# Loading k ahead of q in the head of an attention and shrink-MLP kernel, and storing its last block in quarters

## Chip, cores and metric

The kernel runs on one core of a Trainium2 chip. The metric is the device time of one execution in microseconds (us), as the median of several runs. A profile is one further execution with the hardware profiler on; its span goes from the first to the last instruction, and the execution's own time is a little longer.

## What is computed

Pooled attention for 8 batches of 8 heads, 576 rows, head width 64, and then a two-layer network without bias whose activation is `h - tanh(h)`:

```python
k_p = k.reshape(B, H, Sp, 8, D).mean(axis=3)      # 576 rows -> 72 pooled rows, v likewise
scores = q @ k_p.T / sqrt(D)
attn = exp(scores - max(scores)); attn /= sum(attn)
x = (attn @ v_p), heads side by side              # 4608 x 512
h = x @ w_in                                      # 512 -> 2048
out = (h - tanh(h)) @ w_out                       # 2048 -> 512
```

Inputs and output are float32; inside the kernel the products are of bf16 operands with float32 sums.

## The kernel before

**Tiling.** The rows are worked on in nine groups of 512: group g below 8 takes rows 0 to 511 of batch g (each partition holds four neighbouring rows, j = 0 to 3), and the ninth, g = 8, takes the 64 left-over rows ("tails") of all eight batches. For a group, TensorE first does the h-products (`h_mms`, 16 units of 128 hidden columns; for group 0 in half-wide pairs, `h_mm_pair`, line 447), ScalarE takes the tanh (`h_act`, line 438) and VectorE subtracts it (line 439) into `gT`; then the products with `w_out` follow (`o_mms`, line 468). The attention of batch g + 1 is fitted between them by a plan written out by hand (`plan`, lines 870 to 900).

**Three groups with seven products.** For g in `SEVEN` = (6, 7, 8) the second product is done as a 2 by 2 block product with seven instead of eight sub-products (`PRODUCTS`, line 530, in the order 4, 2, 7, 1, 6, 5, 3; each in two row blocks b = 0 and 1). It needs four sums of quarters of `gT`, S1 to S4 (`g_sum`, line 527). Products 4, 7, 1, 6, 5 and 3 run on in the same two PSUM banks, one for each b, and what is in the bank is copied out in between (`evacuate`, lines 554 to 572): so the copy after product 1 must have read the bank before product 6 adds to it. S2 and S4 are made on VectorE, S1 on GpSimd (line 960). `finish_11` (line 578) adds a last term to a quarter of the output, on GpSimd. `store_half` (line 593 for g = 8) stores columns `C1` (0 to 255) or `C2` (256 to 511), or both, of half hf of the rows, in two transfers.

**The head.** Everything before the steady state is written out by hand from line 605 to line 753, and each engine takes its instructions in that order. The loads of k and q of batch 0 are split into pieces: k in tiles of 128 rows, t = 0 to 4 (t = 4 has 64 rows, 128 KB; two tiles have 512 KB), q in pairs of j (512 KB for two). SyncE and ScalarE have issue queues of their own for them; v, the weights and batch 1's k and q are issued by GpSimd, which converts on the way where the target is bf16: v of batch 0 after the load of k tiles 0 and 1 (`after`, line 637), chunks 1 to 3 of `w_in` after the last step of pooling k (line 672). VectorE pools k (`pool_k`, lines 209 to 215); TensorE turns the pooled k and the q tiles by products with an identity (`turn`, line 272), and ScalarE or VectorE copies them out (`k_place`, line 246; `q_turn_pe`, line 652). Scores (`s_mms`, line 291) go to PSUM; `s_shift` (lines 303 and 306) takes the maximum and subtracts it on VectorE, and `s_exp` (line 342) takes one exponential over all eight heads. The other way, `s_max` with `s_exp_heads` (lines 311 to 332), gives ScalarE the negated maximum as a bias and takes one exponential for each head, straight from PSUM. E is turned on TensorE and copied out (`e_turn_pe`, line 361), multiplied with v (`av_mms`, line 378), normalised (lines 399 and 400) and turned again (`x_turn_pe`, line 417). `fill` (line 599) issues products of zeros that nothing reads.

**Batch 1 in the head.** GpSimd pools k of batch 1 (`pool_k(1, nc.gpsimd)`, line 736, about 6 us) and then converts q of batch 1 tile by tile (line 738). TensorE turns those q tiles from the ninth step of the loop at line 743 on (line 750).

Of the kernel before, what the change touches and what calls it, by code (L numbers as in the profile page):

```python
# [15 lines left out]
B, H, S, D = 8, 8, 576, 64  # L16
POOL = 8
G = S // POOL
DM, DFF = 512, 2048
NHP = H // 2  # L20
R = 4
QA = 128 * R
# [4 lines left out]
NG = 9  # L27
NT = 5
# [10 lines left out]
def kernel(  # L39
# [20 lines left out]
    def flat(b0, n):  # L60
        return PS[:, b0 : b0 + 2, :].rearrange("p k c -> p (k c)")[:, 0:n]
# [63 lines left out]
    def load_rows(src, dst, b, t0=0, t1=NT, eng=None):  # L125
        eng = eng or nc.sync
        r = []
        n1 = min(t1, 4)
        if t0 < n1:
            r.append(  # L130
                eng.dma_start(
                    out=dst[:, t0:n1, :],
                    in_=src[b, 128 * t0 : 128 * n1, :].rearrange("(t p) n -> p t n", p=128),
                )
            )
        if t1 == NT:
            r.append(eng.dma_start(out=dst[0:64, 4, :], in_=src[b, 512:NK, :]))
        return r

    def load_q(b, dst, j0=0, j1=R, eng=None):  # L140
        return (eng or nc.sync).dma_start(
            out=dst[:, :, j0:j1, :],
            in_=q[b, :, 0:QA, :].rearrange("h (p j) d -> p h j d", j=R)[:, :, j0:j1, :],
        )
# [51 lines left out]
    def after(lds, dep):  # L196
        for ld in lds:
            tc.add_manual_dep(
                ld.ins,
                dep.ins.name,  # L200
                mybir.DependencyInfo(mybir.DependencyClass.Sync, mybir.DependencyReason.DATA),
            )


    def pool_k(b, eng, t0=0, t1=NT):
        r = k_raw[b % 2].rearrange("p t (j d) -> p t j d", d=D)[:, t0:t1, :, :]
        kd = kds[b % 2][:, t0:t1, :, :]
        n = t1 - t0
        eng.tensor_tensor(  # L209
            out=r[:, :, 0:4, :], in0=r[:, :, 0:4, :], in1=r[:, :, 4:8, :], op=ALU.add  # L210
        )
        eng.tensor_tensor(
            out=r[:, :, 0:2, :], in0=r[:, :, 0:2, :], in1=r[:, :, 2:4, :], op=ALU.add
        )
        return eng.tensor_tensor(
            out=kd,
            in0=r[:, :, 0:1, :].to_broadcast([128, n, 2, D]),
            in1=r[:, :, 1:2, :].to_broadcast([128, n, 2, D]),
            op=ALU.add,
        )  # L220
# [38 lines left out]
    def q_cast(b, eng, j0=0, j1=R):  # L259
        eng(  # L260
            out=q_bf[b % 2][:, j0:j1, :, :].rearrange("p j h d -> p h j d"),
            in_=q_raw[b % 2][:, :, j0:j1, :],
        )
# [35 lines left out]
    def s_shift(banks):  # L299
        sc = two(banks, 4 * G).rearrange("p k (h c) -> p k h c", c=G)  # L300
        mx = work.tile([128, 2, 4, 1], FP32, name="mx", tag="mx")
        sh = work.tile([128, 2, 4, G], FP32, name="sh", tag="sh", bufs=4)
        nc.vector.reduce_max(  # L303
            out=mx.rearrange("p k h o -> p k (h o)"), in_=sc, axis=AX.X
        )
        nc.vector.tensor_tensor(  # L306
            out=sh[:, :, :, :], in0=sc, in1=mx.to_broadcast([128, 2, 4, G]), op=ALU.subtract
        )
        return sh
# [25 lines left out]
    def slot(n):  # L335
        return E_ps[n // 2 % 2], ET_ps[n // 2 % 2], n % 2
# [3 lines left out]
    def s_exp(sh, sl):  # L340
        E, ET, e = sl
        nc.scalar.activation(  # L342
            out=E[:, e, :, :].rearrange("p t c -> p (t c)")[:, 0:NK],
            in_=sh.rearrange("p k h c -> p (k h c)"),
            func=ACT.Exp,
            scale=SCALE,
        )
# [233 lines left out]
        o = o_hs[1][:, :, C2]  # L581
        eng.tensor_tensor(out=o, in0=o, in1=n0, op=ALU.subtract)

    def store_half(g, hf, cols=slice(0, DM), engs=(nc.sync, nc.sync)):
        o = o_hs[hf]
        if g < B:
            blk = out[g * S : g * S + QA, :].rearrange("(p j) m -> p j m", j=R)
            nc.sync.dma_start(out=blk[:, 2 * hf : 2 * hf + 2, cols], in_=o[:, :, cols])
            return
        tl = out.rearrange("(n t) m -> t n m", t=S)[QA:S, :, :]  # L590
        for e in range(2):
            n = 4 * hf + e
            engs[e].dma_start(
                out=tl[:, n : n + 3 : 2, cols], in_=o[64 * e : 64 * e + 64, :, cols]
            )

    def fill(n, bank, cols=512):
        for _ in range(n):
            nc.tensor.matmul(  # L599
                PS[:, bank, 0:cols], lhsT=zeros[:, 0:128], rhs=zeros[:, 0:cols], start=True, stop=True  # L600
            )
# [2 lines left out]
    ve, se, ge = nc.vector.tensor_copy, nc.scalar.copy, nc.gpsimd.tensor_copy  # L604
    nc.vector.memset(zeros[:, :], 0.0)
    nc.vector.memset(k_raw[0][64:128, 4, :], 0.0)
    k0 = load_rows(k_rows, k_raw[0], 0, 0, 2)
    load_q(0, q_raw[0], 0, 2, nc.scalar)
    k0 += load_rows(k_rows, k_raw[0], 0, 4, NT, nc.scalar)
    k0 += load_rows(k_rows, k_raw[0], 0, 2, 4)  # L610
    load_q(0, q_raw[0], 2, 4)
    nc.vector.memset(v_bf[0][64:128, 4, :], 0.0)
    nc.vector.memset(v_bf[1][64:128, 4, :], 0.0)
# [20 lines left out]
    nc.gpsimd.memset(mask[64:128, 4, :, :], 0.0)  # L634
    for i in range(3):
        nc.gpsimd.tensor_scalar_mul(VB[i][:, :, :, D:D1], mask[:, :, :, :], float(POOL))
    after(load_rows(v_rows, v_bf[0], 0, eng=nc.gpsimd), k0[0])
    w1_dmas = [load_w1(0)]
    nc.gpsimd.memset(k_raw[1][64:128, 4, :], 0.0)

# [1 line left out]
    def k_turn_pe(b, t0, t1, kps):  # L642
        for t in range(t0, t1):
            turn(kps[:, t * 128 : (t + 1) * 128], kds[b][:, t, :, :].rearrange("p a d -> p (a d)"))

    def q_turn_pe(b, j, bank, eng):
        for m in range(NHP):
            turn(
                PS[:, bank, m * 128 : (m + 1) * 128],
                q_bf[b % 2][:, j, 2 * m : 2 * m + 2, :].rearrange("p h d -> p (h d)"),  # L650
            )
        eng(out=qTs[b][:, j, :, :].rearrange("p m c -> p (m c)"), in_=PS[:, bank, :])

    def v_pool_pe(b, bank):
# [8 lines left out]
            )  # L663
        return vps

    pool_k(0, nc.vector, 0, 2)
    pool_k(0, nc.vector, 4, NT)
    pooled = pool_k(0, nc.vector, 2, 4)
    for c in range(1, 4):
        w1_dmas.append(load_w1(c))  # L670
# [4 lines left out]
    load_w2(0)  # L675
    load_w2(1)
    q_cast(0, se, 0, 2)
    q_cast(0, se, 2, 4)
    kps = flat(4, NT * 128)
    k_turn_pe(0, 0, 2, kps)  # L680
    k_turn_pe(0, 4, NT, kps)
    fill(3, 7)
    k_turn_pe(0, 2, 4, kps)
    k_place(0, kps[:, 0:NK], (ve, se))
    q_turn_pe(0, 0, 6, se)
    q_turn_pe(0, 1, 7, se)
    fill(2, 0)
    s_mms(s_block(0, 0), (0, 1))
    sh = [s_shift((0, 1))]
    s_mms(s_block(0, 1), (2, 3))  # L690
    sh.append(s_shift((2, 3)))
    vps = v_pool_pe(0, 6)
    v_place(0, vps, nc.vector)
    s_exp(sh[0], slot(0))
    fill(3, 7)
    e_turn_pe(slot(0), 4, se)
    s_exp(sh[1], slot(1))
    q_turn_pe(0, 2, 0, ve)
    fill(2, 7)
    e_turn_pe(slot(1), 2, se)  # L700
    q_turn_pe(0, 3, 1, se)
    av_mms(slot(0), av_block(0), (6, 7))
    xs = [x_pair(), x_pair()]
# [161 lines left out]
    for g in range(1, NG):  # L865
# [68 lines left out]
        for i in range(NHID):  # L934
            bk = HB[i // 2 % 3][i % 2] if g in SEVEN else i % 6
            h_mms(g, i, bk)
            if g in SEVEN and i == 15:
                for it in plan.pop(-1, ()):
                    step(*it)
            if i % 2:  # L940
                h_act(i - 1, bk - 1)
                if g in SEVEN:
                    if i in (3, 5) and carry:
                        carry.pop(0)()
                    for n, i0 in {13: [(3, 0)], 15: [(3, 4)]}.get(i, ()):
                        g_sum(n, i0, i0 + 4)
            for it in plan.get(i - NHID, ()):
                step(*it)
            if more and i in (13, 15):
                q_cast(nb + 1, se, i - 13, i - 11)  # L950
        for u in range(14 if g in SEVEN else 0):
            n, b = PRODUCTS[u // 2], u % 2
            product(n, b)
            evacuate(n, b, nb is not None)
            for it in plan.get(u, ()):
                step(*it)
                run_late()
            if u == 2:
                dep = g_sum(2, 0, NQ)
                after([g_sum(1, 0, 4, nc.gpsimd), g_sum(1, 4, NQ, nc.gpsimd)], dep)  # L960
            if u == 8:
                g_sum(4, 0, NQ)
            if b == 0:
                continue
            if n == "1":
                finish_11(nc.gpsimd, nb is not None)
                if g == NG - 1:
                    store_half(g, 0, C1)
            elif g == NG - 1 and n == "5":
                store_half(g, 1)  # L970
            elif g == NG - 1 and n == "3":
                store_half(g, 0, C2, (nc.sync, nc.scalar))
            elif n in "53":
                if n == "5" and nb is not None:
                    finish_22(nc.gpsimd)
                store_half(g, 0 if n == "3" else 1)
        if g in SEVEN and tail is not None:
            carry += [lambda i=tail: tail_values(i), lambda i=tail: x_turn_dma(x_tl, B, i, 1)]
        for u, (tb, qd) in enumerate(() if g in SEVEN else UNITS):
# [51 lines left out]
```

## Time and profile before

| what | value |
|---|---|
| median of three runs | 306.02 us (305.19 to 307.4) |
| the profiled execution | 306.24 us, its span 304.2 us |
| TensorE busy | 287.7 us, 95% of the span |
| VectorE, ScalarE, GpSimd busy | 202.8, 145.0 and 135.4 us |
| TensorE busy from 0 to 42 us | 33.77 us |
| TensorE busy from 100 to 220 us | 120 us of 120 |
| first h-product of group 0 | 22.27 us |
| TensorE's last products begin | 296.01 us |
| last store issued | 299.4 us |

How to read it: TensorE, VectorE, ScalarE and GpSimd are called PE, DVE, ACT and POOL in the rows, PEld is TensorE's loading of weights, SP is SyncE; a name with q, such as SPq, is that engine's queue of issuing instructions. A row of the timeline has its start, its duration (both in us), engine, line of the kernel, operation, written tile `<-` read tiles, shapes, a count, and in brackets how long the engine sat idle before and what ended that. A granted clock of 1.00 is TensorE's full clock.

### The profile page before, as it was taken

To read this page: it belongs to the slowest core of one execution; us is meant where nothing else is said; L and a number is where in the kernel's file an instruction comes from. 1 tells how busy PE (TensorE), PEld (TensorE's weight loads), DVE (VectorE), ACT (ScalarE), POOL (GpSimd) and SP (SyncE) were. 2 spreads that over 40 slices of the span, in tenths; PEclk is the share of its full clock that TensorE was granted. 3 is DMA by queue.
4 is the path that set the end of the run, shared out by engine and by line. 5 is a ranking of instruction groups with operands and counts; after the bars stand their busy time and mean duration, and the time that the engine had idled before them with its cause. 6 is when DMAs were issued, how large, how long until landed. Compare 5 with 4: busy or idle time off the path is not lost.

```text
span 304.2 us, 4875 instructions
## 1 busy us (share of the span) xinstructions
PE 287.7 (95%) x1885; PEld 164.0 (54%) x1885; DVE 202.8 (67%) x283; ACT 145.0 (48%) x199; POOL 135.4 (45%) x112
## 2 busy tenths in 40 slices
PE   5779989899999999999999999999999999999991
PEld 1357865444454455445544454455447854874681
DVE  4586866549853993398329942986699847656861
ACT  2457755347523762366237623672366336416520
POOL 7544918308810692088107910791062920250080
PEclk9599999999999999999999999999999999999998
DMA  7999996789899999896799799959825540021005
GB/s 226 224 218 319 207 290 161 136 254 331 169 218 186 357 180 192 251 314 114 177 254 322 136 155 270 337 63 219 241 65 72 91 160 17 2 99 43 1 0 138
DMA packets 85383, 54.84 MB, mean 180 GB/s; under 512 B 60240, under 2 KB 73168, under 8 KB 85360
## 3 DMA queue, kind: packets, MB, share of 16 engines
q1 hardware_dynamic: 77696, 44.84, 58.7%
q0 software_dynamic: 6400, 8.91, 14.2%
q10 hardware_dynamic: 1264, 0.79, 0.9%
q8 instruction: 14, 0.23, 0.3%
q14 instruction: 9, 0.07, 0.1%
HBM read 36.70 MB, written 9.44 MB: 152 GB/s over the span
## 4 chain that ended last, share of the span: by engine, by line
PE 80%; DVE 10%; DMA 3%; ACT 3%; issue 1%; ACTq 0%; DVEq 0%
PE PS L425 31%; PE PS L468 26%; PE PS L545 11%; PE PS L378 4%; DVE gT L439 3%; PE PS L447 3%; PE PS L291 3%; DMA k_raw<-in_k_dram 2%; DVE sh L306 2%; DVE mx L303 2%; PE PS L272 2%; DMA xT<-x_sb 1%; PE PS L599 1%; DVE x_sb L400 1%; ACT E L342 1%
## 5 line engine op out<-in xcount | busy, mean ns | idle before, releaser
L439 DVE TENSOR_TENSOR gT<-PS,t_sb 128x1024 bf16<-128x1024 f32 x64 | 77.1, 1220 | 42.8 <-ACT t_sb L438 42.8
L425 PE MATMUL PS<-xT,w1b 128*128 128x512 bf16 x448 | 100.8, 379 | 1.0 <-DMA xT<-x_sb 0.9
L468 PE MATMUL PS<-w2b,gT 128*128 128x512 bf16 x384 | 89.8, 379 | 0.2 <-ACT v_sm L782 0.2
L438 ACT ACTIVATE t_sb<-PS 128x1024 f32<-128x1024 f32 x64 | 65.6, 1024 | 49.8 <-PE PS L425 48.4
L425 PEld LDWEIGHTS <-w1b 128*128 128x128 bf16 x512 | 49.1, 98 | 57.6 <-issue 1.9
L468 PEld LDWEIGHTS <-gT 128*128 128x128 bf16 x384 | 35.3, 98 | 37.7 <-issue 0.5
L224 POOL TENSOR_TENSOR v_raw<-v_raw 128x1280 f32<-128x1280 f32 x6 | 17.4, 2906 | 40.8 <-DMA v_raw<-in_v_dram 40.8
L489 ACT COPY o_h<-PS 128x512 f32<-128x512 f32 x22 | 12.8, 584 | 45.9 <-PE PS L468 45.8
L527 POOL TENSOR_TENSOR q_raw<-gT 128x1024 bf16<-128x1024 bf16 x6 | 12.6, 2122 | 44.3 <-PE PS L545 38.5
L303 DVE TENSOR_REDUCE mx<-PS 128x8 f32<-128x576 f32 x36 | 26.9, 748 | 5.8 <-PE PS L291 5.8
L342 ACT ACTIVATE E<-sh 128x576 bf16<-128x576 f32 x32 | 21.8, 680 | 18.5 <-DVE sh L306 18.5
L306 DVE TENSOR_TENSOR sh<-PS,mx 128x576 f32<-128x576 f32 x36 | 27.3, 757 | 1.2
L400 DVE TENSOR_TENSOR x_sb<-PS,rden 128x512 bf16<-128x512 f32 x32 | 22.1, 691 | 1.1
L399 DVE RECIPROCAL rden<-PS 128x8 f32<-128x8 f32 x36 | 7.3, 204 | 22.8 <-PE PS L378 22.7
L209 POOL TENSOR_TENSOR k_raw<-k_raw 128x1280 f32<-128x1280 f32 x7 | 20.3, 2904 | 0.1
L545 PEld LDWEIGHTS <-q_raw 128*128 128x128 bf16 x192 | 18.5, 98 | 2.6 <-DVE q_raw L527 0.4
L246 POOL COPY KB<-kT 64x288 bf16<-64x288 bf16 x12 | 5.1, 422 | 28.6 <-DMA kT<-kd 22.6
L260 ACT CAST q_bf<-q_raw 128x1024 bf16<-128x1024 f32 x14 | 14.4, 1038 | 5.6 <-DMA q_raw<-in_q_dram 5.6
L378 PEld LDWEIGHTS <-ET 128*128 128x128 bf16 x192 | 13.2, 98 | 5.3 <-ACT ET L361 0.8
L378 PE MATMUL PS<-VB,ET 128*128 128x130 bf16 (+2 forms) x192 | 15.8, 221 | 0.2 <-ACT ET L361 0.2
L447 PE MATMUL PS<-xT,w1b 128*128 128x256 bf16 x128 | 15.3, 273 | 0.7 <-ACT xT L417 0.7
L545 PEld LDWEIGHTS <-gT 128*128 128x128 bf16 x144 | 13.9, 98 | 2.0
(95 smaller groups left out, 294.4 us busy)
## 6 DMA issues: line engine op xcount, KB each, us to landing
k_raw<-in_k_dram SPq DMA_DIRECT2D x14, 512.0 KB, 8.5
out_dram<-o_h SPq DMA_DIRECT2D x26, 256.0 KB, 3.1
v_raw<-in_v_dram SPq DMA_DIRECT2D x12, 512.0 KB, 5.0
q_raw<-in_q_dram SPq DMA_DIRECT2D x11, 512.0 KB, 7.0
w1b<-in_moe_w_in_dram POOLq DMA_DIRECT2D x4, 512.0 KB, 8.9
q_raw<-in_q_dram POOLq DMA_DIRECT2D x2, 1024.0 KB, 14.8
w2b<-in_moe_w_out_dram POOLq DMA_DIRECT2D x4, 512.0 KB, 18.9
out_dram<-o_h SPq DMA_DIRECT2D x4, 512.0 KB, 2.8
```

The lines of the kernel that those rows point to most:

```text
L209: eng.tensor_tensor(out=r[:, :, 0:4, :], in0=r[:, :, 0:4, :], in1=r[:, :, 4:8, :], op=ALU.add)
L303: nc.vector.reduce_max(out=mx.rearrange("p k h o -> p k (h o)"), in_=sc, axis=AX.X)
L306: nc.vector.tensor_tensor(out=sh[:, :, :, :], in0=sc, in1=mx.to_broadcast([128, 2, 4, G]), op=ALU.subtract)
L342: nc.scalar.activation(out=E[:, e, :, :].rearrange("p t c -> p (t c)")[:, 0:NK], in_=sh.rearrange("p k h c -> p (k h c)"), func=ACT.Exp, s ...
L378: nc.tensor.matmul(PS[ps, banks[half], D1 * h : D1 * (h + s1 - s0)], lhsT=ET[:, t, c0 : c0 + (ps.stop - ps.start)], rhs=VB[kb][:, t, s0:s1 ...
L400: nc.vector.tensor_tensor(out=x_sb, in0=ps[:, :, :, 0:D], in1=rden.to_broadcast([128, 2, 4, D]), op=ALU.mult,)
L425: nc.tensor.matmul(PS[:, bank, :].rearrange("p (j c) -> p j c", j=R), lhsT=w1b[:, fb, i * 128 : (i + 1) * 128], rhs=xT_of(g)[:, :, fb, :], ...
L438: nc.scalar.activation(out=t_sb[:, :, :], in_=ps, func=ACT.Tanh)
L439: nc.vector.tensor_sub(out=gT[:, i : i + 2, :], in0=ps, in1=t_sb[:, :, :])
L447: h_mm_last[0] = nc.tensor.matmul(PS[:, bank, 256 * s : 256 * s + 256].rearrange("p (j c) -> p j c", j=2), lhsT=w1b[:, fb, (2 * n + s) * 1 ...
L468: nc.tensor.matmul(PS[:, bank, 0 : c1 - c0], lhsT=gT[:, i, tb * 128 : (tb + 1) * 128], rhs=w2b[:, i, c0:c1], start=(i == 0), stop=(i == NH ...
L545: nc.tensor.matmul(ps, lhsT=A[:, i, 128 * b : 128 * b + 128], rhs=B_[:, i, :], start=(n in "24" and i == 0), stop=(i == NQ - 1), skip_grou ...
```

## The change

The loads of batch 0 are issued in another order: k tile 4 first on ScalarE's queue; k tiles 0 and 1, k tiles 2 and 3, q tiles 0 and 1 and q tiles 2 and 3 on SyncE's. Pooling and turning k start with tile 4. Of the zero products after the first nine, three of ten stay. The second q tile is copied out on VectorE, and q tiles 2 and 3 are converted there instead of on ScalarE. The first score block's exponential is taken head by head with the maximum as bias; the second block keeps `s_shift`. Pooling v comes after both exponentials in the program, and both E are turned one after the other. For g = 7 and 8 all sums S2, S1 and S4 are made on VectorE right after the last `h_act`. For g = 8 `finish_11` goes to VectorE, and the output is stored in quarters, the last one in two parts.

```diff
-    def store_half(g, hf, cols=slice(0, DM), engs=(nc.sync, nc.sync)):
-        o = o_hs[hf]
-        if g < B:
-            blk = out[g * S : g * S + QA, :].rearrange("(p j) m -> p j m", j=R)
-            nc.sync.dma_start(out=blk[:, 2 * hf : 2 * hf + 2, cols], in_=o[:, :, cols])
-            return
+    def store_half(g, hf):
+        blk = out[g * S : g * S + QA, :].rearrange("(p j) m -> p j m", j=R)
+        nc.sync.dma_start(out=blk[:, 2 * hf : 2 * hf + 2, :], in_=o_hs[hf][:, :, :])
+
+    def store_part(hf, cols, b0, b1, engs=(nc.sync, nc.sync)):
         tl = out.rearrange("(n t) m -> t n m", t=S)[QA:S, :, :]
         for e in range(2):
-            n = 4 * hf + e
+            n = 4 * hf + 2 * b0 + e
             engs[e].dma_start(
-                out=tl[:, n : n + 3 : 2, cols], in_=o[64 * e : 64 * e + 64, :, cols]
+                out=tl[:, n : n + 2 * (b1 - b0) - 1 : 2, cols],
+                in_=o_hs[hf][64 * e : 64 * e + 64, b0:b1, cols],
             )
...
-    k0 = load_rows(k_rows, k_raw[0], 0, 0, 2)
-    load_q(0, q_raw[0], 0, 2, nc.scalar)
-    k0 += load_rows(k_rows, k_raw[0], 0, 4, NT, nc.scalar)
+    k0 = load_rows(k_rows, k_raw[0], 0, 4, NT, nc.scalar)
+    k0 += load_rows(k_rows, k_raw[0], 0, 0, 2)
     k0 += load_rows(k_rows, k_raw[0], 0, 2, 4)
+    load_q(0, q_raw[0], 0, 2)
     load_q(0, q_raw[0], 2, 4)
...
-    after(load_rows(v_rows, v_bf[0], 0, eng=nc.gpsimd), k0[0])
+    after(load_rows(v_rows, v_bf[0], 0, eng=nc.gpsimd), k0[1])
...
+    pool_k(0, nc.vector, 4, NT)
     pool_k(0, nc.vector, 0, 2)
-    pool_k(0, nc.vector, 4, NT)
     pooled = pool_k(0, nc.vector, 2, 4)
...
     q_cast(0, se, 0, 2)
-    q_cast(0, se, 2, 4)
     kps = flat(4, NT * 128)
+    k_turn_pe(0, 4, NT, kps)
     k_turn_pe(0, 0, 2, kps)
-    k_turn_pe(0, 4, NT, kps)
-    fill(3, 7)
+    fill(2, 7)
     k_turn_pe(0, 2, 4, kps)
     k_place(0, kps[:, 0:NK], (ve, se))
     q_turn_pe(0, 0, 6, se)
-    q_turn_pe(0, 1, 7, se)
-    fill(2, 0)
+    q_turn_pe(0, 1, 7, ve)
+    q_cast(0, ve, 2, 4)
     s_mms(s_block(0, 0), (0, 1))
-    sh = [s_shift((0, 1))]
+    ng = s_max((0, 1))
     s_mms(s_block(0, 1), (2, 3))
-    sh.append(s_shift((2, 3)))
+    sh = [None, s_shift((2, 3))]
+    s_exp_heads((0, 1), ng, slot(0))
+    s_exp(sh[1], slot(1))
+    fill(1, 7)
     vps = v_pool_pe(0, 6)
     v_place(0, vps, nc.vector)
-    s_exp(sh[0], slot(0))
-    fill(3, 7)
     e_turn_pe(slot(0), 4, se)
-    s_exp(sh[1], slot(1))
+    e_turn_pe(slot(1), 2, se)
     q_turn_pe(0, 2, 0, ve)
-    fill(2, 7)
-    e_turn_pe(slot(1), 2, se)
     q_turn_pe(0, 3, 1, se)
     av_mms(slot(0), av_block(0), (6, 7))
...
                     for n, i0 in {13: [(3, 0)], 15: [(3, 4)]}.get(i, ()):
                         g_sum(n, i0, i0 + 4)
+                    if i == 15 and nb is None:
+                        for n in (2, 1, 4):
+                            g_sum(n, 0, NQ)
...
-            if u == 2:
+            if nb is not None and u == 2:
                 dep = g_sum(2, 0, NQ)
                 after([g_sum(1, 0, 4, nc.gpsimd), g_sum(1, 4, NQ, nc.gpsimd)], dep)
-            if u == 8:
+            if nb is not None and u == 8:
                 g_sum(4, 0, NQ)
-            if b == 0:
-                continue
-            if n == "1":
-                finish_11(nc.gpsimd, nb is not None)
-                if g == NG - 1:
-                    store_half(g, 0, C1)
-            elif g == NG - 1 and n == "5":
-                store_half(g, 1)
-            elif g == NG - 1 and n == "3":
-                store_half(g, 0, C2, (nc.sync, nc.scalar))
-            elif n in "53":
-                if n == "5" and nb is not None:
-                    finish_22(nc.gpsimd)
-                store_half(g, 0 if n == "3" else 1)
+            if g == NG - 1:
+                if n == "1" and b:
+                    finish_11(nc.vector)
+                    store_part(0, C1, 0, 2)
+                elif n == "6" and b:
+                    store_part(1, C1, 0, 2)
+                elif n == "5" and b:
+                    store_part(1, C2, 0, 2, (nc.sync, nc.scalar))
+                elif n == "3":
+                    store_part(0, C2, b, b + 1, (nc.sync, nc.scalar))
+            elif b:
+                if n == "1":
+                    finish_11(nc.gpsimd, nb is not None)
+                elif n in "53":
+                    if n == "5" and nb is not None:
+                        finish_22(nc.gpsimd)
+                    store_half(g, 0 if n == "3" else 1)
```

## The prediction

> **What bounds the kernel now.** I read the page first: TensorE is busy for 95% of the span, so only where it idles can this change act.
>
> ```profile
> PE   5779989899999999999999999999999999999991
> PEclk9599999999999999999999999999999999999998
> DMA  7999996789899999896799799959825540021005
> ```
>
> The digits of PE (7.6 us each) fall short in the first slices and in the last one. So I read the head and the tail, first by the windows view (PE busy, PEld, DVE, ACT, POOL, then granted clock, DMA share, GB/s).
>
> ```profile
> 6.00:8.00 2.00, 0.28 (x2) 0.11 (x2) 0.35 (x1) 0.79 (x1) 1.87 (x4) 1.00 1.09 297
> 8.00:10.00 2.00, 0.13 (x2) 0.13 (x3) 1.20 (x4) 0.26 (x1) 0.00 (x0) 0.59 1.23 259
> 12.00:14.00 2.00, 2.00 (x15) 1.10 (x13) 0.28 (x1) 1.47 (x3) 2.00 (x4) 0.50 1.24 205
> 14.00:16.00 2.00, 2.00 (x14) 1.38 (x12) 1.90 (x3) 0.35 (x1) 2.00 (x3) 0.70 1.24 201
> ```
>
> TensorE has nothing to do from 6 to 10 us, its clock is halved from 8.4 to 15.2 us, and the transfers are at their limit (share above 1). Then the timeline, head first.
>
> ```profile
> 8.74 0.43 DVE L209 TENSOR_TENSOR k_raw<-k_raw 128x256 f32<-128x256 f32 x1 [2.38 <-DMA k_raw<-in_k_dram]
> 22.27 1.03 PE L447 MATMUL PS<-xT,w1b 128*128 128x256 bf16 x8 [0.67 <-ACT xT L417]
> 27.41 0.74 POOL L192 DMA_DIRECT2D w2b<-in_moe_w_out_dram  x1 [2.56 <-DMA k_raw<-in_k_dram]
> 34.31 2.29 POOL L260 CAST q_bf<-q_raw 128x512 bf16<-128x512 f32 x4
> 36.77 0.39 PE L272 MATMUL PS<-ident,q_bf 128*128 128x128 bf16 x4
> ```
>
> k tile 4 lands at 8.7 us and holds the scores; the first h-product starts at 22.27. GpSimd waits for batch 1's k until 27.41, pools it, and converts batch 1's q from 34.31: each of the four takes 0.61, so the first is there at 34.92, and TensorE turns it at 36.77, 1.85 later. From 30 to 40 us TensorE is busy throughout. Last the tail.
>
> ```profile
> 288.78 1.22 DVE L527 TENSOR_TENSOR q_raw<-gT,q_raw 128x2048 bf16<-128x2048 bf16 x1
> 290.17 4.20 POOL L527 TENSOR_TENSOR q_raw<-gT 128x1024 bf16<-128x1024 bf16 x2 [19.66 <-PE PS L545]
> 292.01 0.42 DVE L572 TENSOR_TENSOR o_h<-PS,k_raw 128x256 f32<-128x256 f32 x1 [2.01 <-PE PS L545]
> 292.51 3.66 PE L545 MATMUL PS<-k_raw,q_raw 128*128 128x256 bf16 x32
> 293.13 2.33 DVE L527 TENSOR_TENSOR q_raw<-gT,q_raw 128x2048 bf16<-128x2048 bf16 x1
> 294.32 2.26 POOL L578 TENSOR_TENSOR o_h<-o_h,k_raw 128x512 f32<-128x512 f32 x1
> 296.61 3.56 SPq L593 DMA_DIRECT2D out_dram<-o_h  x5
> 297.96 0.42 DVE L572 TENSOR_TENSOR o_h<-PS,k_raw 128x256 f32<-128x256 f32 x1 [0.45 <-PE PS L545]
> ```
>
> The last copy ends at 298.38, but SyncE, held by GpSimd's addition until 296.6, issues stores one after the other until about 300.1, and the transfers run until about 302.7 (the windows view has 225 GB/s up to 302.5, 96 up to 303).
>
> **The change, part by part. Head, loads.** All of k and q of batch 0 come in 2.23 MB; by the DMA view 0.27 MB had come by 3 us, 0.90 by 5, 1.84 by 8, and the last packets at 9.5. The sum stays, the order changes. With k alone at some 0.36 MB/us (355 to 437 GB/s in the rows just before 3 us) tile 4 is there at about 3.3, tiles 0 and 1 at 4.2, 2 and 3 at 5.7; q at 0.29 MB/us (287 near 9 us): tiles 0 and 1 at 7.4, 2 and 3 between 9.5 and 10.5, later if v, now issued about 0.6 earlier, takes a share. SyncE issues four loads of 0.46 instead of three, ScalarE one instead of two: its table load moves forward by 0.5 and costs nothing, since ScalarE then waits for q.
>
> **Head, k and q.** VectorE pools tile 4 (1.03), tiles 0 and 1 (1.61), tiles 2 and 3 (1.60) from 3.3 on without a gap but for the landing: done at 7.6 instead of 11.3. Turn 0.3, the two copies of k 0.45 and 0.39: KB at 8.9 instead of 12.7. ScalarE's q cast (1.04) ends at 8.45, first q tile turned and copied (0.4 + 0.58) by 9.55, scores by 10.0 instead of 14.0.
>
> **Head, what VectorE gains.** Ahead of the maximum now stand the copy of the second q tile (0.68) and the cast of q tiles 2 and 3, which waits for that last load. Behind this wait stand the maximum, the second block's two steps, v's placing and the copy of q tile 2, and ScalarE and TensorE wait for them. No row shows this cast on VectorE: from below the 128x512 float addition, 0.69, from above the 128x1024 subtraction, 1.22; I take 1.0, near ScalarE's 1.04. So the maximum starts at about 11.2 (10.9 to 11.7) and ends at 11.95, the scaling of eight columns 0.2 (the reciprocal of eight, 204 ns).
>
> **Head, exponentials.** Eight of 72 columns replace a subtraction (0.76) and one of 576 (0.68). Rows for one: 0.20 (one column) to 0.37 (256 columns); between them 0.25, so 2.0 in all (1.6 to 3.0), against 1.44: plus 0.6, taken from the path only for the first block. The Trainium skill, ScalarE: Activation LUTs, What ACT_TABLE_LOAD costs, speaks against this edit: a bias from a pointer adds about 93 ns to each. By its formula and its overlap of 93 ns eight would take about 2.0 us, and the sum stays. First E at 14.2 instead of 16.3, the second (already shifted at 13.6) at 14.85 instead of 18.2. Turns 0.45 and copies 0.69 each on ScalarE: 15.5 and 16.2. Pooling v (landing at 12.9, TensorE 1.25, placing 1.15) is ready at 15.4. From there the rows of before: products 0.5, normalising 0.9 for each block, turn 0.4, copy 0.59: the first h-product at about 19.2 instead of 22.27, 3.1 us earlier.
>
> **Head, what is late next.** Of these 3.1, TensorE can keep only what batch 1's q allows. Its landing hangs on the bytes ahead of it: GpSimd's queue is at its limit (share 1.24) from 9.5 on with v, all of w_in and k, and these are not fewer. Issuing chunks 1 to 3 of w_in 3.7 us earlier does not shorten that. So the first turn can start at 34.92 + 0.1 instead of 36.77: 1.7 us, and no more. Chunk 3 of w_in (13.1 + 10.7 = 23.8) and the first of w_out (34 at the latest) are in time. **Head: minus 1.7**; bounds 0 (all lost to q or the clock) and 3.1 (batch 1's k as much earlier).
>
> **Fills.** Seven zero products go; they stood in TensorE's waits and cost nothing themselves. Their cover was the clock. Before, TensorE was nearly idle from 5.2 to 8.4, and the clock fell. Now turns, two fills, q and scores keep it busy for some 20% of that time; before, 0.28 of 3.2 us brought the halving, and 1.59 of 2 us (the window from 20 to 22) kept the full clock. I take the full clock, as waits are now about 1 us at most. By the Trainium skill, TensorE: Matmul & The Clock Gate, Part 1, the clock halves after an idle window of about 3.4 us and returns after a busy one; the trace agrees as far as 8.4 to 15.2 us is two such windows. By that rule the waits are too short to halve it.
>
> **Sums on VectorE, g = 7 and 8.** S2, S1 and S4 run without a gap: from 288.78, three of 1.22 and gaps of 0.03 end at 292.5, so the copy after product 1 runs to 292.95 instead of 292.43, and product 6 waits on its bank: 0.5. For g = 7 the same from 262.74: 266.92 against 266.47, 0.5. S4's 2.33 beside GpSimd goes, but nothing waited for it. **Plus 0.5 for each.** Group 7's GpSimd work is off the path.
>
> **Last stores.** The addition (GpSimd 2.26) becomes one on VectorE, 0.69 by the 128x512 float row, done at 294.2: its two stores go out 2.4 earlier, in VectorE's gap before product 5's copy. SyncE issues seven at 0.62, ScalarE three at 0.71, and none has a queue before it: the last pair at 298.9 (0.5 later copy) instead of 299.4. Bytes followed issue by 1.3 before; the last 128 KB then start at 300.2 and end, at 200 to 280 GB/s, at 300.8 to 301.3, against 302.7: minus 1.6 with product 6's wait already in it. With group 7's 0.5: **tail minus 1.1** (minus 0.6 to minus 1.6).
>
> **Sum**: minus 1.7 minus 1.1 = minus 2.8. The profiled execution (306.24, of which 304.2 is the span) is 0.22 above the median; from it 303.4, from the median of 306.02, 303.2.
>
> **Rivals.** *k of batch 1 lands earlier too*, because earlier issue fills the 313 GB/s stretch from 5 to 8 us. For it: v is issued earlier; against it: a share above 1 already. Head minus 3.1, 301.8.
>
> *The clock halves as before.* Against it the short waits, for it that 20% lies in an untested gap. Half speed adds about 1.8 to the chain (v's pooling 0.8, products with v 0.5, turns and scores 0.5): 1.3 of 3.1 are left. Until 22 us it also slows one h pair (eight at 213 instead of 109 ns, 0.83): head minus 0.5, 304.4.
>
> *The clock stays halved into the h-products*: this is the other side. Each pair costs another 0.83, so from the third or fourth pair on (about 26 us) it eats 1.3 and the tail's 1.1; to 28.6 us some five pairs give plus 2.9 minus 1.3 minus 1.1: 306.5, and a further window 308.2. For it: 57% busy was not enough to raise the clock between 8.4 and 11.8; against it: these pairs run back to back.
>
> *The load order brings nothing*, because VectorE stands in line for q tiles 2 and 3: this decides only if they land after 12 us, and at 13.4 the head's gain is gone: 304.9. Against it: before they landed at 10.1 behind the same bytes.
>
> **How the numbers follow.** Forecast 0.58, k earlier 0.10, clock halved briefly 0.15, halved long 0.09, q late 0.08. A measurement of this kernel tells about 1% (3.06 us) from no change. Faster by that means under 302.96: all of k earlier, and a good third of the forecast (302.4 to 304.2): 0.32. Slower, over 309.1: only the longest halving and what I have not seen, 0.06. The rest 0.62. The range, 301.6 to 306.4, leaves out the longest halving and a tail at its best with k earlier.
>
> **What would show it.** Right: first h-product near 19, an idle stretch of about 1.4 us ahead of the first turn of batch 1's q near 35, GpSimd's wait for k still ending near 27.4; product 6 waiting about 0.5 on line 572 twice; last issue about 0.5 before its time of before. Wrong: a granted clock of 0.5 beyond 10 us, no idle stretch near 35, or the first maximum after 13 us.

## The result and the profile after

The changed kernel takes 301.31 us (median of 4 runs, 301.21 to 301.52), against 306.12 (305.19 to 307.4) for the kernel before on the same chip: 4.8 us less by the medians. The ratio of the two is 0.9853, with an interval of 0.9828 to 0.9879, which is 4.5 us less (3.7 to 5.3). The forecast was 303.2, in a range that began at 301.6: the sign is right, the time lies at the lower edge of the range, and the gain is 4.8 instead of 2.8. The profiled run took 301.21 with a span of 299.5; before it was 306.24 with 304.2. So the two traces differ by 4.7 us, and the question is where these lie.

The 40 slices of the page of after first, then its windows view over the head (columns as before).

```profile
PE   5789989999999999999999999999999999999994
PEclk9699999999999999999999999999999999999999
```

```profile
6.00:8.00 2.00, 0.23 (x2) 0.10 (x2) 1.90 (x6) 0.00 (x0) 1.70 (x3) 1.00 1.17 305
8.00:10.00 2.00, 1.20 (x9) 0.71 (x10) 1.44 (x4) 1.04 (x1) 0.24 (x1) 0.79 1.24 262
14.00:16.00 2.00, 2.00 (x14) 1.32 (x13) 1.27 (x2) 1.87 (x7) 1.79 (x3) 0.51 1.24 206
16.00:18.00 2.00, 2.00 (x32) 1.75 (x30) 1.86 (x4) 1.54 (x3) 0.35 (x1) 1.00 1.24 205
```

The clock was granted at 0.50 from about 9.2 to 16.0 us: the halving is still there. TensorE had been busy for only 0.23 of the two microseconds from 6 to 8, and for 0.95 of the 3.4 from 5.8 to 9.2. Now the timeline of after, head.

```profile
5.34 0.43 DVE L209 TENSOR_TENSOR k_raw<-k_raw 128x256 f32<-128x256 f32 x1 [2.04 <-DMA k_raw<-in_k_dram]
12.85 2.34 PE L658 MATMUL PS<-v_raw,ident 128*128 128x320 bf16 x8
13.26 1.80 ACT L326 ACTIVATE E<-PS,ng 128x72 bf16<-128x72 f32 x8 [1.82 <-DVE ng L318]
20.09 1.03 PE L447 MATMUL PS<-xT,w1b 128*128 128x256 bf16 x8 [0.67 <-ACT xT L417]
27.61 0.74 POOL L192 DMA_DIRECT2D w2b<-in_moe_w_out_dram  x1 [3.59 <-DMA k_raw<-in_k_dram]
34.52 2.29 POOL L260 CAST q_bf<-q_raw 128x512 bf16<-128x512 f32 x4
35.19 0.40 PE L272 MATMUL PS<-ident,q_bf 128*128 128x128 bf16 x4 [0.43 <-POOL q_bf L260]
```

k tile 4 is there at 5.3 instead of 8.7 us, all of k is pooled at 9.45 instead of 11.3, the first h-product starts at 20.09 instead of 22.27. GpSimd's wait for batch 1's k still ends at 27.61 (27.41 before), and TensorE now waits, 0.43 us, for the converted q: the first turn of batch 1's q starts at 35.19 instead of 36.77. Last the tail of after.

```profile
287.33 1.22 DVE L527 TENSOR_TENSOR q_raw<-gT 128x2048 bf16<-128x2048 bf16 x1
288.47 1.22 DVE L527 TENSOR_TENSOR q_raw<-gT,q_raw 128x2048 bf16<-128x2048 bf16 x1
289.61 0.42 DVE L572 TENSOR_TENSOR o_h<-PS,k_raw 128x256 f32<-128x256 f32 x1
290.08 3.65 PE L545 MATMUL PS<-k_raw,q_raw 128*128 128x256 bf16 x32
290.66 0.69 DVE L578 TENSOR_TENSOR o_h<-o_h,k_raw 128x512 f32<-128x512 f32 x1
291.38 5.07 SPq L593 DMA_DIRECT2D out_dram<-o_h  x7
294.22 2.27 ACTq L593 DMA_DIRECT2D out_dram<-o_h  x3
295.51 0.42 DVE L572 TENSOR_TENSOR o_h<-PS,k_raw 128x256 f32<-128x256 f32 x1 [0.45 <-PE PS L545]
```

Product 6 starts at 290.08, just behind the copy of 289.61, which follows the last sum. It starts 1.89 us behind the start of product 1 instead of 1.74, in group 7 as in group 8: a wait of 0.15. The addition is done at 291.35, stores go out from 291.38 instead of 296.61, and from the end of the last copy (295.93) to the end of the span there are 3.57 us instead of 5.82.

The 4.7 us, laid out along the two traces by TensorE's landmarks:

| stretch | before | after | difference | forecast |
|---|---|---|---|---|
| start to first turn of batch 1's q | 36.77 | 35.19 | -1.6 | -1.7 |
| from there to group 1's first h-product | 24.20 | 23.29 | -0.9 | 0 |
| from there to group 7's first product | 198.52 | 198.28 | -0.2 | 0 |
| two waits of product 6 (groups 7, 8) | 0 | 0.3 | +0.3 | +1.0 |
| end of last copy to end of span | 5.82 | 3.57 | -2.25 | -2.1 |

The last line of forecasts splits the tail of the prediction: its -1.6 held one product-6 wait of 0.5.

### The profile page after: what moved, and what is told of

The parts are those of the page before. It is cut to its first block, busy times and chain, and to the rows that moved or that the text cites. A ratio compares the mean times of both kernels' runs of the same rounds, so it can differ in the third digit from the quotient of the medians.

```text
span 299.5 us, 4873 instructions
## 1 busy us (share of the span) xinstructions
PE 286.9 (96%) x1878; PEld 164.0 (55%) x1878; DVE 204.2 (68%) x288; ACT 144.6 (48%) x204; POOL 124.3 (42%) x107
## 4 chain that ended last, share of the span: by engine, by line
PE 77%; DVE 8%; DMA 7%; POOL 3%; issue 1%; ACT 1%; ACTq 0%; DVEq 0%; POOLq 0%
PE PS L425 32%; PE PS L468 26%; PE PS L545 11%; DMA k_raw<-in_k_dram 6%; PE PS L378 4%; DVE gT L439 3%; PE PS L291 3%; DVE sh L306 1%; DVE mx L303 1%; POOL k_raw L209 1%; DMA xT<-x_sb 1%; POOL w1b L187 1%; ACT t_sb L438 1%; PE PS L447 1%; DVE k_raw L209 1%
## 5 line engine op out<-in xcount | busy, mean ns | idle before, releaser
L468 PEld LDWEIGHTS <-gT 128*128 128x128 bf16 x384 | 35.4, 98 | 37.3
L342 ACT ACTIVATE E<-sh 128x576 bf16<-128x576 f32 x31 | 21.2, 682 | 16.2 <-DVE sh L306 16.2
L303 DVE TENSOR_REDUCE mx<-PS 128x8 f32<-128x576 f32 x35 | 26.2, 748 | 3.6 <-PE PS L291 3.6
L306 DVE TENSOR_TENSOR sh<-PS,mx 128x576 f32<-128x576 f32 x35 | 26.5, 757 | 1.2
L246 POOL COPY KB<-kT 64x288 bf16<-64x288 bf16 x12 | 5.1, 422 | 27.7 <-DMA kT<-kd 27.4
L260 ACT CAST q_bf<-q_raw 128x1024 bf16<-128x1024 f32 x13 | 13.4, 1038 | 5.4 <-DMA q_raw<-in_q_dram 5.4
L291 PE MATMUL PS<-KB,qT 128*128 128x144 bf16 x128 | 13.4, 232 | 1.8 <-ACT KB L246 0.9
L291 PEld LDWEIGHTS <-qT 128*128 128x128 bf16 x128 | 10.3, 100 | 8.8 <-issue 1.6
```

The source lines that it names most:

```text
L291: nc.tensor.matmul(PS[ps, banks[m // 2], KP * (m % 2) : KP * (m % 2) + KP], lhsT=qT[:, m, :], rhs=KB[kb][:, m, :], start=True, stop=True,)
L303: nc.vector.reduce_max(out=mx.rearrange("p k h o -> p k (h o)"), in_=sc, axis=AX.X)
L306: nc.vector.tensor_tensor(out=sh[:, :, :, :], in0=sc, in1=mx.to_broadcast([128, 2, 4, G]), op=ALU.subtract)
L342: nc.scalar.activation(out=E[:, e, :, :].rearrange("p t c -> p (t c)")[:, 0:NK], in_=sh.rearrange("p k h c -> p (k h c)"), func=ACT.Exp, s ...
L468: nc.tensor.matmul(PS[:, bank, 0 : c1 - c0], lhsT=gT[:, i, tb * 128 : (tb + 1) * 128], rhs=w2b[:, i, c0:c1], start=(i == 0), stop=(i == NH ...
```

## The experiments

**Each part alone.** The theory: head and tail add up, and the head gives more than the forecast's 1.7. Two kernels have one half of the diff each, and the kernel before ran once more. The ratio of each run here is to the kernel before, measured beside it.

e1 is the changed kernel with the sums of groups 7 and 8 and the last group's addition and stores as before; e2 is the kernel before with exactly these changed; e3 is the kernel before, without an edit. The edit of e1 against the changed kernel (e2 has the same lines with the signs turned, against the kernel before):

```
-                    if i == 15 and nb is None:
-                        for n in (2, 1, 4):
-                            g_sum(n, 0, NQ)
...
-            if nb is not None and u == 2:
+            if u == 2:
...
-            if nb is not None and u == 8:
+            if u == 8:
...
-                    finish_11(nc.vector)
-                    store_part(0, C1, 0, 2)
+                finish_11(nc.gpsimd, nb is not None)
+                if g == NG - 1:
+                    store_half(g, 0, C1)
...
-                    store_part(1, C2, 0, 2, (nc.sync, nc.scalar))
+                store_half(g, 1)
...
-                    store_part(0, C2, b, b + 1, (nc.sync, nc.scalar))
+                store_half(g, 0, C2, (nc.sync, nc.scalar))
```

> All edits of the head, sums and stores at the end as before. Theory (the head gives 1.6 us by the first turn of batch 1's q and somewhat more by 61 us, the rest comes from the end): 2.5 to 3.0 us less than before, the first h-product of group 0 near 20.1 us, the first turn of batch 1's q near 35.2 us. Rival (the head gives only the 1.7 us of its cap, and the further 1.1 us between 37 and 259 us were an accident of the one profile of before): 1.4 to 1.9 us less.

> Head as before, the sums for g = 7 and 8 on VectorE, the addition on VectorE and the quarter stores as in the change. Theory: 0.15 us lost at product 6 in each of the two groups, 2.2 us won after the last copy, so 1.8 to 2.2 us less than before. Rival (the forecast's 0.5 us for each wait and 1.6 at the end): 1.1 us less.

> The kernel before once more, for a second profile of it. If the waits of 0.2 us at line 468 near 46 us, of 0.9 us for xT near 61 us and the later 0.2 us are its own, they are there again; if they were chance, they are gone and its first h-product of group 2 comes nearer to 24 us after the first turn of batch 1's q instead of 24.2.

Measured: the head alone 303.41 us, ratio 0.9915 (0.9896 to 0.9935), 2.65 less; the tail alone 303.87, 0.9926 (0.9907 to 0.9945), 2.2 less. Together 4.85, as the whole change. The kernel before once more took 306.09 (a single run): there the stretch from the q turn to group 1 is 24.21, as in the first profile (24.20), while its first turn of q starts at 36.38 instead of 36.77. So by these two profiles of before, the head's first stretch is worth 1.2 to 1.6. It scatters: the first turn of q is at 35.63 with the head alone and at 36.21 with the tail alone, only 0.6 apart. The 0.9 of the second is no scatter: it is 24.25 with the tail alone and 23.28 with the head alone.

**Where the 0.9 is.** Timeline of after, then of before, the same two instructions:

```profile
41.42 0.76 DVE L303 TENSOR_REDUCE mx<-PS 128x8 f32<-128x576 f32 x1 [1.05 <-PE PS L291]
58.48 1.89 PE L425 MATMUL PS<-xT,w1b 128*128 128x512 bf16 x8 [0.40 <-DMA xT<-x_sb]
```

```profile
43.39 0.76 DVE L303 TENSOR_REDUCE mx<-PS 128x8 f32<-128x576 f32 x1 [1.46 <-PE PS L291]
60.97 6.20 PE L425 MATMUL PS<-xT,w1b 128*128 128x512 bf16 x28 [0.94 <-DMA xT<-x_sb]
```

From the first turn of q, the first maximum of batch 1 starts 6.23 us later in after and 6.62 in before, though its score products start 5.7 later in both: a pause of 0.4. And TensorE waits 0.40 instead of 0.94 for the transposes of x. Nothing in the diff touches either. But the diff allocates a new small tile, `ng`, ahead of `x_sb`, and so moves `x_sb` in SBUF (and the work tiles behind it), from byte 206208 of a partition (128 past a multiple of 256) to 206336 (a multiple of 512). The next two kernels take the kernel before and change one thing each: the address alone, by a tile that nothing uses, and the number of VectorE's instructions ahead, by two more tiny memsets.

In e7, then in e8:

```
+    work.tile([128, H], FP32, name="ng", tag="ng", bufs=4)
     ve, se, ge = nc.vector.tensor_copy, nc.scalar.copy, nc.gpsimd.tensor_copy
```

```
-    nc.vector.memset(warm[:, :], 0.0)
+    for _ in range(3):
+        nc.vector.memset(warm[:, :], 0.0)
```

> The kernel before, in which only the 128 bytes for the negated maxima are set aside before the other work tiles, as the changed head does by using them first; no instruction is added. It moves the tiles x_sb from byte 384 to byte 0 of a 512-byte row. Theory (the transfers that turn x take 2.7 instead of 3.2 us to land because of where x_sb lies): 2.7 us, TensorE's wait for xT near 61 us 0.4 instead of 0.9, 0.5 to 1.0 us less than before. Rival (they are faster because of the head's other order): 3.2 us and no change.

> The kernel before with two more tiny memsets on VectorE at the start, so that its later instructions stand two places further on, as in the changed kernel. Theory (the pause of 0.4 us ahead of the first maximum of batch 1 near 43 us lies in where that instruction stands in VectorE's stream): the maximum starts 0.52 instead of 0.92 us after its scores, 0.4 us less. Rival (it lies in the tiles' places or in the head's order): 0.92 us and no change.

The address alone: 305.39 us, 0.9967 (0.9954 to 0.9981), 0.6 to 1.4 less. The view of line 408's transposes between 45 and 62 us, first before, then with the address moved:

```profile
  PE PS L425: 0.9, 1
DMA to landing us min/median/max: 3.2/3.2/3.3
```

```profile
  PE PS L425: 0.4, 1
DMA to landing us min/median/max: 2.7/2.8/2.8
```

The same transposes land half a microsecond sooner, and the wait falls by as much: this half of the 0.9 is shown. It agrees with the Trainium skill, DMA: Bandwidth & Descriptors, How a descriptor splits into AXI transactions, by which a descriptor that does not start on a multiple of 256 bytes pays for extra beats; that section does not speak of transposes.

The pause stayed in this kernel (6.64). The tiny memsets took it away (6.21), at 305.38 us, 0.9988 (0.9972 to 1.0004): too little to be seen in the time. That the number of instructions on VectorE decides is not shown, since e11 below has the same number as before and no pause either. The pause is there in four profiles (before twice, the tail alone, the moved address) and away in all others: its cause stays open.

**The cap at 35 us.** The prediction held that the head can gain only as much as batch 1's q is sooner. Two kernels move what stands ahead of it on GpSimd's queue: a load of w_out put behind the conversion, and batch 1's k put ahead of two chunks of w_in.

In e6, then in e9:

```
     load_w2(2)
-    load_w2(3)
     pool_k(1, nc.gpsimd)
     for j in range(R):
         q_cast(1, ge, j, j + 1)
+    load_w2(3)
```

```
         if c == 1:
             after(w1_dmas[1:], pooled)
+            load_rows(k_rows, k_raw[1], 1, eng=nc.gpsimd)
-    load_rows(k_rows, k_raw[1], 1, eng=nc.gpsimd)
```

> The changed kernel with chunk 3 of the second weights issued by GpSimd after pooling and converting batch 1's k and q instead of before. Theory (the head is held by GpSimd's work on batch 1, so what it does ahead of that counts): the first conversion ends 0.75 us earlier, TensorE's wait of 0.43 us ahead of the first turn of batch 1's q goes, 0.4 to 0.7 us less than the changed kernel. Rival (that wait is hidden elsewhere or the last weights now come late): no change, or more.

> The changed kernel with batch 1's k loaded between chunks 1 and 2 of the first weights instead of behind chunk 3. Theory (the landing of batch 1's k, by way of GpSimd, is what holds TensorE near 35 us): GpSimd pools it some 4 us earlier, TensorE's wait ahead of the first turn of batch 1's q goes, that turn comes 14.5 us after the first h-product as in the kernel before, 0.3 to 0.8 us less than the changed kernel. Rival (the weights behind it now come late): a new wait of TensorE at line 447 between 25 and 35 us and no gain.

e6 took 301.08 us, 0.9843 (0.9827 to 0.9858): TensorE's wait is gone and the turn starts at 34.79, 0.40 earlier, but the time falls by 0.2 to 0.3 only, within the intervals of both. e9 took 300.71 (300.52 to 300.96), 0.983 (0.9803 to 0.9856), the fastest of all, though its interval overlaps that of after. Its timeline, GpSimd:

```profile
24.27 2.89 POOL L209 TENSOR_TENSOR k_raw<-k_raw 128x1280 f32<-128x1280 f32 x1
30.36 2.28 POOL L260 CAST q_bf<-q_raw 128x512 bf16<-128x512 f32 x4
```

Pooling starts 4.15 us sooner than in after (28.42), the conversion 4.16, and the turn, at 34.58, no longer waits: it comes 0.61 sooner, where TensorE's own work puts it (14.5 us behind the first h-product, as in the kernel before). That is the cap seen from both sides.

**The clock.** With the cap moved away by e9, a head at full clock might show in the time. So e9 once more, with more zero products to keep TensorE busy: 12 instead of 9 at the start, 5 (new) between k's turns, 5 instead of 2, and 4 instead of 1.

```
-    fill(9, 7)
+    fill(12, 7)
...
     k_turn_pe(0, 4, NT, kps)
+    fill(5, 7)
     k_turn_pe(0, 0, 2, kps)
-    fill(2, 7)
+    fill(5, 7)
     k_turn_pe(0, 2, 4, kps)
...
-    fill(1, 7)
+    fill(4, 7)
```

> The same, with 12, 5, 5 and 4 products of zeros in the waits of the head instead of 9, none, 2 and 1. Theory (with the hold at batch 1's k gone, the half clock of the head, seen in turns of 0.11 us and in 2.3 us for pooling v, is worth its price): scores and pooling of v at full speed, first h-product near 19 us, 0.7 to 1.2 us less than with the early k alone. Rival (the landing of v near 12.8 us and VectorE hold the head): first h-product at 19.7 or later, less than 0.4 us.

Its timeline, TensorE:

```profile
12.72 1.25 PE L658 MATMUL PS<-v_raw,ident 128*128 128x320 bf16 x8
19.58 1.03 PE L447 MATMUL PS<-xT,w1b 128*128 128x256 bf16 x8 [0.67 <-ACT xT L417]
```

The clock stays full (v's pooling takes 1.25 instead of 2.34), the first h-product comes at 19.58 instead of 20.07. In the trace this half microsecond holds up to group 7, but the time is 300.87 us (299.96 to 302.23), 0.9836 (0.9808 to 0.9863), no less than e9: whether it is worth anything is open. So the halving cost about 0.5 us at the first h-product, not the 1.8 that the rival priced. In this trace the head waits next for VectorE's steps, one behind the other, with v's landing (pooling starts at 12.72) close behind.

**Load order without the reordering.** Only the order of loads, pooling and k's turns, on the kernel before; exponentials, turns and fills as before.

```
-    k0 = load_rows(k_rows, k_raw[0], 0, 0, 2)
-    load_q(0, q_raw[0], 0, 2, nc.scalar)
-    k0 += load_rows(k_rows, k_raw[0], 0, 4, NT, nc.scalar)
+    k0 = load_rows(k_rows, k_raw[0], 0, 4, NT, nc.scalar)
+    k0 += load_rows(k_rows, k_raw[0], 0, 0, 2)
     k0 += load_rows(k_rows, k_raw[0], 0, 2, 4)
+    load_q(0, q_raw[0], 0, 2)
...
-    pool_k(0, nc.vector, 0, 2)
     pool_k(0, nc.vector, 4, NT)
+    pool_k(0, nc.vector, 0, 2)
...
-    k_turn_pe(0, 0, 2, kps)
     k_turn_pe(0, 4, NT, kps)
+    k_turn_pe(0, 0, 2, kps)
```

> The kernel before with the new order of the loads, of pooling k and of its turns alone; both q casts and q copies stay on ScalarE, the exponentials and fills as before. Theory (k first brings most of the head's gain, but ScalarE now stands at the cast of q tiles 2 and 3 before it can place k): k pooled near 9.5 instead of 11.3 us, first h-product some 1.2 us earlier than before, 0.8 to 1.3 us less than before, with x_sb and VectorE's stream where they were. Rival (the head's other edits bring the gain): less than 0.5 us.

305.36 us, 0.9983 (0.9958 to 1.0008): nothing that can be told from zero, though the interval reaches to 1.3 less. What speaks against the theory is the trace. Its timeline:

```profile
13.40 2.34 PE L657 MATMUL PS<-v_raw,ident 128*128 128x320 bf16 x8
15.53 1.09 PE L599 MATMUL PS<-zeros 128*128 128x512 bf16 x3
16.46 0.44 PE L272 MATMUL PS<-ident,E 128*128 128x128 bf16 x5
17.53 0.69 ACT L342 ACTIVATE E<-sh 128x576 bf16<-128x576 f32 x1
```

The first exponential ends at 15.42, but its turn stands in TensorE's order behind v's pooling and three zero products, until 16.46. The second exponential stands in ScalarE's order behind the copy of the first turn, until 17.53. The first h-product comes at 22.24 us, as before (22.27), and not 1.2 earlier. Earlier k is cashed in only by the new order behind it.

**Eight exponentials or one.** e9 with the first block shifted on VectorE and one exponential of 576 columns, the tile `ng` kept in place.

```
-    ng = s_max((0, 1))
+    sh = [s_shift((0, 1))]
...
-    sh = [None, s_shift((2, 3))]
-    s_exp_heads((0, 1), ng, slot(0))
+    sh.append(s_shift((2, 3)))
+    s_exp(sh[0], slot(0))
```

> The changed kernel with batch 1's k early, as in the run before (so that the head is not held at batch 1's q), and with the first block's exponential taken as one over shifted scores again; the 128 bytes for the negated maxima stay set aside, so the x tiles lie as in the changed kernel. Theory (the first products with v wait for v's placing on VectorE near 16.5 us, not for E): the first E 0.5 us earlier, the second 0.3 later, first h-product within 0.3 us of 20.1, time within 0.3 us of the run with the early k. Rival (the exponentials by head win, as they bring the second E sooner): 0.5 us more; or they cost the 0.6 us of the forecast: 0.5 us less.

300.88 us, 0.9837 (0.9816 to 0.9859), against 0.983 for e9: the same. The first E is there at 14.56 instead of 15.04, the second at 16.01 instead of 15.61, and the first h-product at 20.28 instead of 20.07. The eight small exponentials give back on the second block what they cost on the first.

**The tail, its two halves.** After with stores in halves, as before, and after with the sums and the addition on GpSimd, as before.

In e4:

```
-                    store_part(0, C1, 0, 2)
-                elif n == "6" and b:
-                    store_part(1, C1, 0, 2)
+                    store_half(g, 0, C1)
...
-                    store_part(1, C2, 0, 2, (nc.sync, nc.scalar))
-                elif n == "3":
-                    store_part(0, C2, b, b + 1, (nc.sync, nc.scalar))
+                    store_half(g, 1)
+                elif n == "3" and b:
+                    store_half(g, 0, C2, (nc.sync, nc.scalar))
```

In e5 the quarters stay:

```
-                    if i == 15 and nb is None:
-                        for n in (2, 1, 4):
-                            g_sum(n, 0, NQ)
...
-            if nb is not None and u == 2:
+            if u == 2:
...
-            if nb is not None and u == 8:
+            if u == 8:
...
-                    finish_11(nc.vector)
+                    finish_11(nc.gpsimd)
```

> The changed kernel with the stores of the last group in halves as before, sums and addition on VectorE as changed. Theory (SyncE's issue is no longer held up once the addition is early, so the quarters matter only by the smaller last pieces): 0.4 to 0.8 us more than the changed kernel. Rival (the quarters are what shortened the end): 1.5 us more or above.

> The changed kernel with S1 and the last addition on GpSimd and S4 later, as before; the quarters stay. Theory (quarters and early addition need each other: SyncE takes its stores in order and stands at the first until GpSimd's addition is done, 2.3 us after the copy of product 1): the last issue on SyncE comes some 1.5 us later than in the changed kernel, 1 to 2 us more; the two waits of 0.15 us at product 6 are gone. Rival (the quarters alone bring the gain): within 0.3 us of the changed kernel.

Halves: 302.88 us, 0.9892 (0.9872 to 0.9912), 1.2 above after by the ratios and 1.6 by the times; between theory and rival. GpSimd's sums: 303.26, 0.9907 (0.9893 to 0.9921), 1.65 and 1.95 above. What SyncE waited for from 285 us on, in the waits view, first halves, then GpSimd's sums (total, times, longest):

```profile
SPq L593 <- DVE o_h L572: 1.8, 2, 1.5
```

```profile
SPq L593 <- POOL o_h L578: 23.8, 1, 23.8
```

With halves SyncE waits up to 1.5 us for product 5's copies while the transfers are nearly idle (share 0.09 from 294 to 295 us, 0.80 in after). With GpSimd's addition its first store goes out at 293.62 instead of 291.38, and the small stores queue up behind it. Added together the two losses, 2.85 to 3.5, exceed the tail's 2.2: each half of the edit is worth more with the other. From these numbers the sums and the addition alone would give about 0.6 to 1.0, the quarters alone about 0.2 to 0.6 (estimates).

## Why the prediction was right or wrong

*The bound and the cap: right.* The head's gain ends at the first turn of batch 1's q: forecast -1.7, measured -1.2 to -1.6, with a wait on `q_bf` in that place and GpSimd's wait for k ending at 27.6. e6 and e9 take the cap away and gain 0.4 and 0.6 at that turn. The forecast idle stretch of 1.4 us became 0.43, since the h-products came later than forecast. That the cap stood within 0.2 of its forecast place is partly luck: it was read from one profile. GpSimd's wait for k ended between 27.4 and 28.3 in the other kernels that keep this load in its place, and at 28.75 in the second profile of the kernel before, where the first converted q is there at 36.26, only 0.12 ahead of its turn.

*The way there: wrong in three steps, hidden by the cap.* The first h-product came at 20.09 instead of 19.2, and the cap left nothing of that in the time, which is luck.
- The landings. Tile 4 was there at 5.3, not 3.3: its 128 KB on ScalarE's queue landed after tiles 0 and 1, which SyncE issued beside it. I had let the queues serve it first and alone. k was pooled at 9.45, not 7.6.
- The clock. "I take the full clock" failed: it was halved from 9.2 to 16.0, behind a stretch of 3.4 us in which TensorE was busy for 0.95 us (28%) and never waited longer than 1.3. A granted clock of 0.5 beyond 10 us was the prediction's own sign of being wrong. The reason given, that the waits are short, does not decide. My text had some 20% busy, and the row of before that this was nearest to (0.28 of 3.2 us, halved) should have decided. The rule that stood beside it (the Trainium skill, TensorE: Matmul & The Clock Gate, Part 1) has the clock halve after an idle window of about 3.4 us; in this trace a window that was 28% busy was enough. The rise at 16.0, behind back-to-back products from 12 us on, agrees with that rule.
- VectorE's cast took 0.68 to 0.91, not 1.0, and the eight exponentials 1.80, not 2.0. Both are small and to the good.

With the clock halved, that rival's arithmetic gave 304.4. It erred by charging half speed to the chain in full, and by a further 0.83 for h-products before 22 us, when the clock had been full again since 16.0.

*What was not in the sum:* -0.9 between the q turn and group 1, which the prediction had put at nothing. About 0.5 is the address of `x_sb` (e7), 0.4 the pause, whose cause is open. The prediction read the diff for instructions alone, not for the tile that it adds.

*Plus 0.5 for each of product 6's waits: mis-sized.* Measured 0.15 each. I spaced the three sums by their length and a gap, 1.25; in the trace of after they start at 286.19, 287.33 and 288.47, 1.14 apart, less than the 1.22 that each lasts. Over three sums that is the missing third of a microsecond, twice 0.35.

*The last stores: right.* -2.25 from the last copy to the end against a forecast of -2.1; quarters and the early addition are both needed for it (e4, e5).

So 301.3 instead of 303.2 is -0.9 (not foreseen), -0.7 (the waits), and about -0.3 in the head, the stores and the groups between, where two profiles of one kernel differ by as much.

## What to carry to other kernels

When a diff adds or resizes a tile, look at what it moves: here an operand of DMA transposes that came to a better boundary was worth 0.6 to 1.4 us, beside 4.8 for the whole change. Before costing an earlier load, follow each engine's written order behind it: with the new loads alone the first h-product stayed where it was, until exponentials, turns and zero products stood in the order in which their data came. And find the next landing behind the edited stretch that the edit does not move, since it caps the gain and hides errors ahead of it; read it in more than one profile, as here it differed by 1.3 us between two profiles of one kernel.

## What the runs showed of the hardware

- DMA transposes of x landed in 3.2 us from a source 128 bytes past a multiple of 256, and in 2.7 from a multiple of 512, with no instruction changed (before and e7).
- TensorE's clock halved behind 3.4 us with 28% of busy time, the longest wait being 1.3 us. In e10, where no 3.4 us between 6.5 and 18 us had less than 2.1 us (62%) busy, it stayed full. Durations, not the clock row, tell the speed: with the head alone the row says 1.00 from 12 to 16 us, yet v's pooling took 2.34 us, as at 0.50 in after.

```profile
12.00:14.00 2.00, 2.00 (x12) 1.25 (x10) 1.84 (x5) 0.73 (x4) 2.00 (x4) 1.00 1.24 206
```

- Back-to-back VectorE sums of 1.22 us start 1.14 apart (after), so a chain of them is shorter than its durations added.
- A pause of 0.4 us ahead of one maximum on VectorE came and went with edits that do not touch it; the runs do not say why.
